# Retention attention with a Mish feed-forward on one core: partition order of the first two tiles' q and k loads, and the place of the first v loads

## The chip, the core and the metric

The kernel runs on one core of a Trainium2 chip. The metric is the device time of one execution in microseconds. Before the change it was 333.55 us, the median of 3 runs (333.04 to 334.23).

A core has TensorE (PE in the profile; its weight loads are PEld), VectorE (DVE), ScalarE (ACT), GpSimd (POOL) and SyncE (SP). Transfers between the off-chip memory and the on-chip buffer run on the core's 16 DMA engines. They are issued here from SP's queue, ACT's queue and POOL's queue.

## What is computed

The inputs are q, k and v of 8 batches, 8 heads, 576 tokens and 64 features, and two weight matrices. The reference, cut to what matters:

```python
scores = (1/sqrt(64)) * q @ k^T                      # per batch and head, 576 x 576
gamma  = 1 - 2 ** (-5 - head)
D[i,j] = gamma ** (i-j) if i >= j else 0
attn   = (scores * D) @ v                            # 576 x 64
x = attn, heads side by side                         # 4608 x 512
h = x @ w_in                                         # 4608 x 2048
g = h * tanh(softplus(h))                            # Mish
out = g @ w_out                                      # 4608 x 512
```

## The kernel before

**Tiles.** The 4608 tokens are cut into 36 chunks of 128, and four chunks make a tile, so there are 9 tiles. Tiles 0 and 1 hold the first 128 tokens of batches 0 to 3 and of batches 4 to 7. They need no state from earlier tokens and have code of their own, the functions whose names begin with `f_`. Chunks 8 to 35 use the general path (`step_p` to `step_o`), with a running state per batch.

**Order of the work.** The schedule is written by hand (`manual_schedule`, L77): every engine executes its instructions in the order in which the program text issues them, and waits only for the data and buffers that it needs.

**First loads of q and k.** `load_rows` (L101) loads q or k of one batch's first 128 tokens, 256 KB, into one plane of a staging buffer with 128 partitions of 512 floats. Eight consecutive tokens of one head go to one partition (2 KB): "(g r)" splits the 128 tokens into g = 16 groups of r = 8. L103 puts the heads outermost, so partition = 16 * head + group. For tile 0 six of these loads are issued from SP (L115: q0, q1, q2, k2, q3, k3) and two from ACT (L117: k0, k1). For tile 1 eight are issued from SP through `load_second_qk` (L105), four when `g1` of tile 0 has reached block f = 6 and four when it has reached f = 12 (L482 to L485). A tiny transfer named `passed` (L484), which reads the result of that block, holds SP's queue until then.

**First loads of v.** `load_first_v` (L110) loads v of one batch's first 128 tokens from POOL's queue, 128 tokens outermost, in pieces of 256 bytes. For batches 0 and 1 it is called at L135, after the distance table `dist`, the identity and `pos`, and before the two causal masks of the general path (`mask`, `mask2`, L137 to L143). The masks are first used by `step_s` (L296), in tile 2.

**From the staging buffer to scores.** `f_cast` (L177) casts two batches of q or k to bf16 and puts them side by side. `f_transpose` (L185) makes eight PE transposes for q and eight for k. Column number c of a transposed block is partition c of the staging buffer; two copies (L192) put the columns into token order per head. `f_scores` (L196) makes q k^T per head and multiplies by the decay `dmask` on DVE. `f_v` (L212) casts v, and `f_out` (L217) multiplies scores by v and copies the result to `xT`. For tile 0 the order is at L434 to L463: casts of batches 0 and 1, their transposes, casts of batches 2 and 3, scores, transposes, outputs, and in between the first four blocks of `g1`.

**POOL's order at the start.** After the masks POOL casts v of batch 0 (L438), which waits for that load, issues the first quarter of w_in (L439), the loads of v 2 and 3 (L441), casts v of batch 1, issues the rest of w_in (L444), casts v of batch 2 (L456), issues w_out (L465), scales v for the states (L467) and then issues v 4 to 7 and the loads of chunks 8 to 11 (L469 to L473).

**Feed-forward.** `g1(t, f)` (L359) multiplies block f of w_in with `xT` of a tile and applies Mish on ACT; there are 16 blocks. `g2_first` (L390) multiplies Mish's result of tile 0 with w_out. Tile 1's attention steps are put between the parts of `g2_first` (L488). From L516 on the general path interleaves the attention of later chunks with `g1` and `g2` of earlier tiles.

Of the kernel before, what the change touches and what calls it, by code (L numbers as in the profile page):

```python
# [17 lines left out]
def kernel(  # L18
# [19 lines left out]
    B, H, S, D = q.shape  # L38
    assert (B, H, S, D) == (8, 8, 576, 64)
    P = 128  # L40
# [59 lines left out]

    def load_rows(queue, t, i, b):  # L101
        queue.dma_start(out=raw[t][i][:, b, :],  # L102
                        in_=(q, k)[i][4 * t + b, :, 0:P, :].rearrange("h (g r) d -> h g (r d)", r=8))  # L103

    def load_second_qk(g):  # L105
        for b in (2 * g, 2 * g + 1):
            for i in range(2):
                load_rows(nc.sync, 1, i, b)

    def load_first_v(b):  # L110
        v0[b] = io.tile([P, H, D], F32, name="vraw", bufs=8)
        nc.gpsimd.dma_start(out=v0[b], in_=v[b, :, 0:P, :].rearrange("h p d -> p h d"))

    for i, b in ((0, 0), (0, 1), (0, 2), (1, 2), (0, 3), (1, 3)):
        load_rows(nc.sync, 0, i, b)  # L115
    for b in range(2):
        load_rows(nc.scalar, 0, 1, b)  # L117
# [14 lines left out]
                   allow_small_or_imprecise_dtypes=True)  # L132
    nc.gpsimd.iota(pos[64:P, 4:5], pattern=[[1, 1]], base=512, channel_multiplier=1,
                   allow_small_or_imprecise_dtypes=True)
    for b in range(2):  # L135
        load_first_v(b)
    mask = consts.tile([P, P], F32)  # L137
    mask2 = consts.tile([P, P], F32)
    nc.gpsimd.memset(mask, 1.0)
# [1 line left out]
                            base=0, pattern=[[1, P]], channel_multiplier=-1)  # L141
    nc.gpsimd.tensor_copy(mask2, mask)
    nc.gpsimd.memset(mask2[0:64, 64:P], 0.0)  # L143
    lg = [math.log(1.0 - 2.0 ** (-5.0 - h)) for h in range(H)]
    dmask = consts.tile([P, H, P], F32)
    for h in range(H):
# [38 lines left out]
    def f_transpose(t, g, copies, tps):  # L185
        for i, name in enumerate(("qb", "kb")):
            for r in range(8):
                nc.tensor.transpose(tps[i][:, r, :], fst[t][name][:, g, r, :, :].rearrange("p x d -> p (x d)"),  # L188
                                    ident)
        for i, name in enumerate(("qb", "kb")):  # L190
            out_t = first.tile([P, H, P], BF16, name=name + "T", bufs=2)
            copies[i](out_t.rearrange("p h (g r) -> p h g r", r=8),  # L192
                      tps[i].rearrange("p r (h g) -> p h g r", h=H))
            fst[t][name, g] = out_t

    def f_scores(t, g):  # L196
# [246 lines left out]
    for i in range(1, 4):  # L443
        load_w_in(512 * i, 512)  # L444
    keep_warm(11)
    f_transpose(0, 0, (act, dve), [ps_h.tile([P, 8, P], BF16, name="hp") for _ in range(2)])
    for i, x in ((0, 0), (0, 1), (1, 0), (1, 1)):
        f_cast(0, i, 1, act, one[x])
    keep_warm(3, ps_sc, "sc")
    f_scores(0, 0)  # L450
    f_transpose(0, 1, (act, act), [ps_st.tile([P, 8, P], BF16, name="st"), ps_o.tile([P, 8, P], BF16, name="ops")])
    f_out(0, 0, act)
    f_out(0, 1, dve)
# [26 lines left out]
    for f in range(4, nF):  # L480
        g1(0, f)
        if f in (6, 12):  # L482
            g = f // 6 - 1
# [5 lines left out]
    for i in range(nF):  # L489
        for step in steps.get(i, "").split():  # L490
            n = int(step[1])
            if step[0] == "T":
                f_transpose(1, n, (dve, act), [ps_sc.tile([P, 2, 8, P], BF16, name="sc")[:, 0] for _ in range(2)])
            elif step[0] == "S":
                f_scores(1, n)
            elif step[0] == "V":
                f_v(1, n, act)
            elif step[0] == "C":
                for j in range(2):
                    f_cast(1, j, n, dve)  # L500
            else:
                f_out(1, n, (dve, act)[n % 2])
        g2_first(i // 4, i % 4)
# [114 lines left out]
```

## Time and profile before

| what | before |
|---|---|
| median of 3 runs | 333.55 us |
| the profiled execution's own time | 335.72 us |
| its span in the profile | 334.0 us |
| PE busy | 306.6 us, 92% of the span |
| PEld, DVE, ACT, POOL busy | 154.6, 137.8, 113.4, 138.8 us |
| mean granted clock of PE | 0.964 |
| DMA traffic | 44.42 MB in 73642 packets |

The profile is one execution. The span is measured from its first to its last event, and the execution's own time is 1.72 us longer. Times inside the profile (a start, a landing) count from the beginning of the span. "Busy" is the time in which an engine executes instructions; a share of DMA is the mean busy share of the 16 DMA engines, so that one half can mean that all are half busy or that half of them are fully busy. It can come out a little above 1. The granted clock is the share of TensorE's full speed that it was given. Queue q1 of the profile carries the DMAs that SP issues, q10 those of ACT, q0 those of POOL, as the issue times and byte counts of the three show.

### The profile page before, as it was taken

The numbers are of one execution on the slowest core, as the hardware profiler recorded it, in microseconds if no ns is written. First come the engines' busy times: TensorE is split into PE (matmuls) and PEld (weight loads), VectorE is DVE, ScalarE is ACT, GpSimd is POOL, SyncE is SP. The second block draws the span as 40 slices with busy tenths as digits, with TensorE's granted clock in tenths as the row PEclk, the third lists the DMA queues.
The fourth block names the chain that finished last, engine by engine and source line by source line (L and its number), as shares of the span: only waits on it lengthen the run. The fifth ranks groups of instructions, "written<-read, shape, count | busy, mean of one in ns | idle before, by whom it ended". The sixth has DMA issues, their size and how long they took to land.

```text
span 334.0 us, 5789 instructions
## 1 busy us (share of the span) xinstructions
PE 306.6 (92%) x2430; PEld 154.6 (46%) x2430; DVE 137.8 (41%) x198; ACT 113.4 (34%) x186; POOL 138.8 (42%) x169
## 2 busy tenths in 40 slices
PE   5568619899999999999999999999999999999996
PEld 1354204445555554545454545455454545444444
DVE  3351003874776474545353545354545433000121
ACT  3376501157623444232322232322222232333300
POOL 5768262919782679482936344452210000000000
PEclk9679956999999999999999999999999999999999
DMA  4899998959985859999999997994061510010022
GB/s 145 239 219 205 252 218 189 180 162 163 163 145 113 150 111 177 200 173 134 179 138 163 152 170 124 154 141 122 31 96 42 87 62 34 31 33 31 31 78 81
DMA packets 73642, 44.42 MB, mean 133 GB/s; under 512 B 58640, under 2 KB 62992, under 8 KB 73616
## 3 DMA queue, kind: packets, MB, share of 16 engines
q0 software_dynamic: 46976, 25.70, 50.0%
q1 hardware_dynamic: 26224, 17.70, 23.8%
q10 hardware_dynamic: 416, 0.66, 0.6%
q8 instruction: 19, 0.31, 0.4%
q14 instruction: 7, 0.06, 0.1%
HBM read 38.80 MB, written 9.44 MB: 144 GB/s over the span
## 4 chain that ended last, share of the span: by engine, by line
PE 84%; DMA 9%; DVE 2%; SPq 1%; ACT 1%; issue 1%; DVEq 0%
PE hp L364 36%; PE ops L379 28%; DMA gT<-in_k_dram 9%; PE hp L379 4%; PE sc L293 2%; PE st L325 2%; PE hp L396 2%; PE sc L345 2%; PE sc L350 2%; SPq L102 1%; DVE kb L182 1%; PE sc L280 1%; PE hp L407 1%; PE ops L396 1%; PE st L396 1%
## 5 line engine op out<-in xcount | busy, mean ns | idle before, releaser
L364 PE MATMUL hp<-xT,w_in_t 128*128 128x512 bf16 (+1 forms) x592 | 144.1, 374 | 1.6 <-DVE xT L231 0.8
L366 ACT ACTIVATE gT<-hp 128x512 bf16<-128x512 f32 (+1 forms) x148 | 86.6, 586 | 155.3 <-PE hp L364 155.1
L379 PE MATMUL ops<-w_out_t,gT 128*128 128x512 bf16 x432 | 110.4, 379 | 0.0
L364 PEld LDWEIGHTS <-w_in_t 128*128 128x128 bf16 x592 | 55.1, 98 | 62.6 <-issue 1.6
L379 PEld LDWEIGHTS <-gT 128*128 128x128 bf16 x496 | 48.3, 98 | 58.0 <-issue 0.8
L415 DVE COPY res<-ops 128x512 f32<-128x512 f32 x28 | 19.3, 688 | 83.3 <-PE ops L379 79.7
L255 POOL DMA_DIRECT2D qraw<-in_q_dram x24 | 22.0, 915 | 51.1 <-DVE qks L265 50.8
L328 DVE TENSOR_TENSOR ssb<-st,diag 128x512 bf16<-128x512 f32 x32 | 21.9, 684 | 47.5 <-PE st L325 47.5
L271 POOL TENSOR_TENSOR vs<-vraw,gv 128x512 bf16<-128x512 f32 x28 | 29.8, 1071 | 20.4 <-issue 13.9
L297 DVE TENSOR_TENSOR sm<-sc,mask 128x1024 bf16<-128x1024 f32 x28 | 33.0, 1214 | 7.1 <-PE sc L293 7.1
L255 POOL DMA_DIRECT2D vraw<-in_v_dram x24 | 21.7, 905 | 8.1 <-DMA qks<-in_k_dram 5.7
L255 POOL DMA_DIRECT2D qks<-in_k_dram x24 | 22.0, 916 | 4.2 <-DMA w_out_t<-in_moe_w_out_dram 1.6
L265 DVE TENSOR_TENSOR qks<-qraw,gq 128x512 bf16<-128x512 f32 x28 | 18.7, 700 | 0.0
L354 DVE CAST xT<-sc 128x512 bf16<-128x512 f32 x24 | 15.3, 680 | 0.0
L379 PE MATMUL hp<-w_out_t,gT 128*128 128x512 bf16 x64 | 15.0, 379 | 0.0
L182 DVE CAST qb<-gT 128x512 bf16<-128x512 f32 (+1 forms) x4 | 2.9, 734 | 26.9 <-DMA gT<-in_q_dram 26.9
L281 ACT COPY qkT<-sc 128x1024 bf16<-128x1024 bf16 x10 | 10.1, 1010 | 8.0 <-PE sc L280 8.0
L259 POOL DMA_DIRECT2D qraw<-in_q_dram x8 | 5.6, 702 | 13.8 <-DVE qks L265 13.8
L188 PEld LDWEIGHTS <-qb 128*128 128x128 bf16 x32 | 2.5, 119 | 17.6 <-DVE qb L182 16.4
L188 PE MATMUL sc<-ident,qb 128*128 128x128 bf16 x16 | 1.6, 263 | 9.8 <-DVE qb L182 9.8
L192 ACT COPY kbT<-sc 128x1024 bf16<-128x1024 bf16 x2 | 2.0, 1012 | 24.8 <-DVE qbT L192 12.5
L396 PEld LDWEIGHTS <-gT 128*128 128x128 bf16 x64 | 6.5, 108 | 8.1 <-issue 2.7
(95 smaller groups left out, 224.8 us busy)
## 6 DMA issues: line engine op xcount, KB each, us to landing
vraw<-in_v_dram POOLq DMA_DIRECT2D x32, 256.0 KB, 7.1
out_dram<-res SPq DMA_DIRECT2D x31, 256.0 KB
qraw<-in_q_dram POOLq DMA_DIRECT2D x24, 256.0 KB, 3.7
qks<-in_k_dram POOLq DMA_DIRECT2D x24, 128.0 KB, 4.4
gT<-in_q_dram SPq DMA_DIRECT2D x8, 256.0 KB
w_in_t<-in_moe_w_in_dram POOLq DMA_DIRECT2D x4, 512.0 KB, 10.3
w_out_t<-in_moe_w_out_dram POOLq DMA_DIRECT2D x4, 512.0 KB, 12.9
gT<-in_k_dram SPq DMA_DIRECT2D x6, 256.0 KB
```

What stands on the lines that cost most here:

```text
L255: nc.gpsimd.dma_start(out=t, in_=src[b, :, ds(P * c, P), :].rearrange("h p d -> p h d"))
L265: nc.vector.tensor_tensor(live[n]["qks"][:, 0], live[n]["q"], gq[:, c, :].unsqueeze(2).to_broadcast([P, H, D]), op=OP.mult)
L271: nc.gpsimd.tensor_tensor(vs, live[n]["v"], gv[:, c, :].unsqueeze(2).to_broadcast([P, H, D]), op=OP.mult)
L281: nc.scalar.copy(qk.rearrange("p i n t -> p (i n) t"), tp)
L297: nc.vector.tensor_tensor(sm.rearrange("p e n i -> p (e n) i"), sc.rearrange("p e n i -> p (e n) i"), m.unsqueeze(1).to_broadcast([P, 2 * ...
L328: nc.vector.tensor_tensor(ssb.rearrange("p e n d -> p e (n d)"), st.rearrange("p n d -> p (n d)").unsqueeze(1).to_broadcast([P, 2, NP * 64 ...
L354: nc.vector.tensor_copy(xts[t][:, :, ts(s, P)], ot)
L364: nc.tensor.matmul(hp[:, cols], lhsT=w_in_t[:, c, ts(f, P)], rhs=xts[t][:, c, cols], start=(c == 0), stop=(c == KC - 1))
L366: nc.scalar.activation(gts[t][:, f, cols], hp[:, cols], AX.Mish)
L379: nc.tensor.matmul(ops, lhsT=gts[t][:, f, ts(s, P)], rhs=w_out_t[:, f, :], start=(f == 0), stop=(f == nF - 1))
L396: nc.tensor.matmul(outs[0, s], lhsT=gts[0][:, f, ts(s, P)], rhs=w_out_t[:, f, :], start=(f == 0), stop=(f == nF - 1))
L415: copy(ot, ops)
```

## The change

Three lines of code change, and two lines move.

1. `load_rows` puts the 16 groups of tokens outermost and the 8 heads within, for all 16 loads of q and k of tiles 0 and 1. The partition is now 8 * group + head. Each piece is still 2 KB and each load still 256 KB.
2. `f_transpose` reads the transposed columns in the new order, "(g h)" instead of "(h g)"; the result in memory is the same.
3. The two calls of `load_first_v` for batches 0 and 1 move behind the four POOL instructions that make the masks.

```diff
     def load_rows(queue, t, i, b):
         queue.dma_start(out=raw[t][i][:, b, :],
-                        in_=(q, k)[i][4 * t + b, :, 0:P, :].rearrange("h (g r) d -> h g (r d)", r=8))
+                        in_=(q, k)[i][4 * t + b, :, 0:P, :].rearrange("h (g r) d -> g h (r d)", r=8))
...
-    for b in range(2):
-        load_first_v(b)
     mask = consts.tile([P, P], F32)
     mask2 = consts.tile([P, P], F32)
     nc.gpsimd.memset(mask, 1.0)
...
     nc.gpsimd.tensor_copy(mask2, mask)
     nc.gpsimd.memset(mask2[0:64, 64:P], 0.0)
+    for b in range(2):
+        load_first_v(b)
...
             copies[i](out_t.rearrange("p h (g r) -> p h g r", r=8),
-                      tps[i].rearrange("p r (h g) -> p h g r", h=H))
+                      tps[i].rearrange("p r (g h) -> p h g r", h=H))
```

## The prediction, made before the changed kernel was run

> **What bounds the kernel now.** I read the page's slices and chain first, then the busy times of chosen stretches, the timeline of the stretches in which PE is not busy, and the traffic of each DMA queue there. Stretches first (us, length, busy time of each engine with its count, granted clock, DMA share, GB/s):
>
> ```profile
> 0.00:8.00 8.00, 4.24 (x11) 1.43 (x11) 3.07 (x23) 2.68 (x4) 4.31 (x16) 1.00 0.48 142
> 8.00:15.00 7.00, 3.68 (x27) 2.24 (x29) 1.93 (x2) 2.06 (x3) 4.84 (x7) 0.51 0.74 222
> 15.00:22.00 7.00, 4.24 (x64) 3.25 (x61) 3.09 (x4) 4.89 (x7) 3.06 (x5) 0.76 1.19 247
> ...
> 38.70:51.60 12.90, 1.87 (x17) 1.61 (x18) 2.28 (x3) 0.60 (x1) 5.68 (x6) 0.64 1.08 220
> 51.60:73.00 21.40, 19.77 (x147) 9.23 (x146) 13.69 (x13) 5.84 (x9) 10.35 (x11) 0.90 0.86 171
> 73.00:283.00 210.00, 210.00 (x1847) 106.09 (x1847) 104.10 (x143) 73.86 (x120) 98.78 (x112) 1.00 0.82 130
> ```
>
> From 73 us on PE is busy for 210.00 of 210.00 us, so whatever brings the work at 73 us forward brings the end forward, and nothing else in the change can. PE's losses lie before 26 us and between 38.7 and 51.6, where it works 1.87 of 12.90 us. The chain of waits says for what:
>
> ```profile
> 4.37 13.63 DMA gT<-in_k_dram
> 18.69 1.05 PE ops L188 x8
> ...
> 34.35 15.58 DMA gT<-in_k_dram
> 50.77 1.04 PE sc L188 x8
> ```
>
> Both long pieces are loads of `load_rows`: the last k of tile 0, landed at 18.0, and the k of tile 1's second batch, landed at 49.95. (The buffer bears the name gT because the staging area is later a gT buffer.) Next, how fast these loads run:
>
> ```profile
> 3.50:5.00 1.50, 1.50 (x6) 0.55 (x5) 0.12 (x2) 1.49 (x2) 1.32 (x4) 1.00 0.53 193
> ...
> 8.00:12.00 4.00, 0.90 (x8) 0.77 (x8) 0.71 (x1) 0.35 (x1) 1.84 (x3) 0.52 0.53 193
> 24.00:32.00 8.00, 7.14 (x56) 4.13 (x55) 1.72 (x3) 4.83 (x11) 7.99 (x9) 1.00 1.24 204
> ```
>
> Between 3.5 and 5 us nothing but q and k moves, many loads are queued, and yet the DMA share stays at 0.53 with 193 GB/s; from 8 to 12 it is the same. A backlog with a share that stands at one half reads as eight engines of sixteen, one for each head of the outermost dimension. POOL's weight loads, with 128 outermost, bring the share to 1.24. So I read the change as doubling the engines of each q and k load, from 8 to 16. The trace has no load with 16 outermost: the bounds are no gain (193 GB/s) and the double (386 GB/s); I take the double, since eight heads gave eight engines and 128 tokens gave all.
>
> The Trainium skill, "DMA: Bandwidth & Descriptors", section "Why a DMA increments its semaphore by 16 and not by 1", says that a DMA uses the largest number of engines up to 16 that divides the slowest dimension of both sides: 8 before, 16 now. Its section "Where 436 GB/s comes from" speaks against the whole double: the memory gives one core about 358 GB/s. By that figure the 2.10 MB of tile 0 take 5.9 us (an estimate from that page) and not 5.4, and the sum would be 0.5 us smaller. Of the stretches of 1 us that I read, the highest is 318 GB/s (15 to 16 us).
>
> **Part 1, tile 0.** Eight loads of 262 KB are 2.10 MB, 10.9 us at 193 GB/s and 5.4 at 386. The timeline of the work behind them:
>
> ```profile
> 10.71 0.78 POOL L86 DMA_DIRECT2D w_in_t<-in_moe_w_in_dram  x1
> ...
> 11.65 0.62 ACT L182 CAST kb<-gT 128x512 bf16<-128x512 f32 x1 [6.28 <-DMA gT<-in_k_dram]
> ...
> 18.02 0.62 ACT L182 CAST kb<-gT 128x512 bf16<-128x512 f32 x1 [1.29 <-DMA gT<-in_k_dram]
> ...
> 20.03 0.61 POOL L214 CAST vb<-vraw 128x512 bf16<-128x512 f32 x1 [3.94 <-DMA vraw<-in_v_dram]
> ...
> 22.68 0.60 ACT L214 CAST vb<-vraw 128x512 bf16<-128x512 f32 x1
> ...
> 26.01 8.36 PE L364 MATMUL hp<-xT,w_in_t 128*128 128x256 bf16 x44 [0.79 <-DVE xT L231]
> ```
>
> By 5.0 us the queues of SP and ACT had moved 0.39 MB. On twice the engines that is 0.78 MB, and 1.24 MB at 6.2 us. Data land about 1 us after the byte counts say (0.26 MB on SP's queue at about 5.6, cast at 6.95). So k1, the fourth of the eight, lands at about 6 instead of 11.65, and the other four, which share the engines with v 0 and 1, between 7.4 and 11.2 instead of 13 to 18. From k1's cast to the scores of batches 0 and 1 took 3.0 us (11.65 to 14.67), then come casts of 0.62, transposes of at most 1.05, copies of 1.01 and 1.22, multiplications of 1.18 each: done one behind the other they bring ACT past the Mish table load (1.28 us, ended 22.56) at about 16.0. That is 6.5 us earlier.
>
> What is late next is v. The masks cost POOL 0.20 + 0.29 + 0.29 + 0.14 = 0.92 us, with gaps 1.13 (4.33 to 5.46), and v's data begin at 6.2 instead of 5.05. v 0 then has q and k beside it on every engine. At half of the 204 GB/s that POOL's queue had alone, its 262 KB take 2.6 us, so it lands at about 9.5 (10.15 before); POOL's cast takes 0.61 and w_in's first quarter is issued near 10.1 (10.71 before). The masks thus cost nothing, since nobody uses them before 73 us and v 0 gains more than they delay it. Behind that quarter stand v 2 and v 3, 1.05 MB in all. They had q and k beside them until 18; now they have the engines to themselves from about 10.5. At 204 to 275 GB/s (24 to 32 us, 12 to 16 us) they need 3.8 to 5.1 us from about 11.8, and land at about 17, with 1 us of lag. v 3's cast on ACT starts at about 17.2 instead of 22.68, and the row at 26.01, from which PE works almost without a gap to 38.7, follows. **Part 1: -5.5 us**, bounds -4 (v 3 at 18.7) and -7 (q and k alone decide). The next quarters of w_in land every 2.6 us (0.52 MB at 204) from about 19.6; g1 needs one per 4 blocks x 0.865 us = 3.5 us, so they hold nothing up.
>
> **Part 2, tile 1.** The loads begin when g1 of tile 0 has reached f = 6 and compete with w_out, v 4 to 7 and the chunk loads:
>
> ```profile
> 32.32 0.63 SPq L102 DMA_DIRECT2D gT<-in_q_dram  x1
> ...
> 36.75 0.58 SPq L484 DMA_DIRECT2D passed<-gT  x1
> ...
> 50.02 0.69 DVE L182 CAST kb<-gT 128x1024 bf16<-128x1024 f32 x1 [1.60 <-DMA gT<-in_k_dram]
> ```
>
> Issued at 32.32, landed at 50.0: 17.7 us for 1.05 MB. SP's queue moved almost nothing until 36 (3.7 us), then 0.40 MB to 41.5, which is 73 GB/s or 9.1 per engine. On 16 engines that is 145 GB/s: 3.7 + 7.2 + 1 of lag = 11.9 us, 5.8 less. If both queues got half of each engine (12 of 24 GB/s), it is 3.7 + 5.5 + 1 = 10.2, 7.5 less. I take 6.2, near the measured rate. PE reaches the end of tile 0's g1 6.4 us after the issue, so it still waits some 4 to 5 us. The second four loads follow at the same rate and land some 19 us after the first issue; their casts stood at 59.4, 27 after it, and come to stand 21 after. They fit, by little. **Part 2: -6.2**, bounds -4 and -7.7.
>
> **Part 3, PE's clock.** The granted clock was 0.50 from 43 to 55, and some ten matmuls after 51.6 took 0.43 us instead of 0.22: 2.1 us. It fell 3.7 us after PE stopped. With a wait of 4 to 5 us, cut by the transposes of q, it may fall or not: I take **-1.0**, bounds 0 and -2.1.
>
> **Nothing.** The copies of L192 keep their 1024 elements per partition, and only the step between columns changes: DVE 1.22, ACT 1.01 us. If they cost or saved a fifth, the eight copies, three on the chain, move the end by 0.7 us. SP's issues keep 0.6 us each. From 73 us on POOL's loads have slack: chunk 11's were issued by 60, and PE needs it at about 84; they also come earlier, since POOL had sat up to 5.7 us on transfers that shared engines with q and k.
>
> **Sum.** -5.5 - 6.2 - 1.0 = -12.7 us on the profiled span of 334.0 (321.3), which its own time exceeds by 1.72. The median of the runs is 333.55, 2.17 below the profiled execution; the difference carries over: 320.8 us.
>
> **The rivals.**
> - *More of it.* Queues share evenly and the wait is too short for the clock to fall: -7 - 7.5 - 2.1 = -16.6, 317.0 us. For it: engines of 24 GB/s were at 9 beside POOL's traffic in a stretch that also ended waits of POOL. Against: all three ends at once. Chance 0.14.
> - *Tile 0 gives little.* v 0 has q and k on all its engines and lands no earlier; w_in and v 2, v 3 follow late, and only 1 to 2 us remain of part 1: -1.5 - 5.8 = -7.3, 326.2 us. For it: POOL's cast of v 0 already waited 4.70 us. Chance 0.16.
> - *The loads stay on eight engines*, because sixteen groups are not spread as I read it. Then only v's delay acts: q and k have the engines alone 1.1 us longer, v 0 comes about 1 later: 333.5 us within 1. Chance 0.04.
> - *Slower.* Pieces of 2 KB from eight distant heads run at half of each engine's rate, so 16 engines carry 193 GB/s, and they take it from v 0 on every engine instead of eight. Then q and k end near 13, v 0 lands near 15, w_in is issued 5 later, v 3 lands near 25 and its cast comes 2 later than 22.68: 335.6 us. It decides where v 0 lands more than about 3 us later than 10.15. Against: the slowest row with all engines, 204 GB/s, is above 193. Chance 0.04.
>
> **Numbers.** My forecast has 0.62. Its own range is 318 to 324. The range for 8 in 10 reaches into the first two rivals: 315.5 to 327.5. Faster by over 0.3% (about what a measurement of this kernel can tell from no change) has 0.62 + 0.14 + 0.16 = 0.92, the same 0.04, slower 0.04.
>
> **What would show it.** DMA share near 1 and over 300 GB/s between 3.5 and 5 us; k1's cast near 6 to 7, the last k's near 11; v 0's cast at 9 to 10; g1's long run from about 20.5; tile 1's k cast about 12 us after its first load's issue; PE busy without a gap from about 60. I am wrong if the share stays at 0.53, if v 0 lands after 11, or if PE waits in the general path because chunk loads come late.

## The result, and the profile after

The changed kernel took 324.64 us, the median of 4 runs, where the old one took 333.44 us: 8.8 us less. The ratio of the two kernels is 0.9717 (95% interval 0.9672 to 0.9762). Ratios here compare only runs that count as fast, which leaves out this kernel's run of 329.06 us and one later run of the old kernel (527.5 us). Measured a second time the changed kernel took 327.21 us against 333.85, a ratio of 0.9781 (0.9730 to 0.9832). The ten runs of these two measurements lie between 323.0 and 329.1 us; their standard deviation is 2.2 us, against 1.1 us for the old kernel's 47 runs (332.2 to 337.3).

The first stretches of the changed kernel's profile, with the columns of before (us, length, busy time of each engine with its count, granted clock, DMA share, GB/s), have the same bounds as the first three rows shown of the old kernel; the last three are cut at the new events:

```profile
0.00:8.00 8.00, 5.14 (x14) 1.75 (x15) 3.92 (x24) 3.30 (x5) 4.50 (x16) 1.00 0.75 191
8.00:15.00 7.00, 6.51 (x59) 4.42 (x56) 3.58 (x3) 4.70 (x7) 3.75 (x6) 1.00 0.79 183
15.00:22.00 7.00, 5.52 (x56) 3.69 (x56) 3.32 (x4) 4.85 (x10) 6.19 (x9) 1.00 1.20 239
...
35.10:41.30 6.20, 1.95 (x18) 1.65 (x18) 2.32 (x3) 0.60 (x1) 0.90 (x1) 0.70 1.14 302
41.30:60.20 18.90, 18.57 (x143) 8.95 (x143) 10.32 (x13) 5.84 (x9) 15.86 (x17) 0.92 1.32 251
60.20:270.50 210.30, 208.72 (x1818) 106.30 (x1848) 104.79 (x143) 74.07 (x120) 98.81 (x112) 1.00 0.83 134
```

The stretch between tile 0's `g1` and `g2_first`, in which PE mostly stands and does little but tile 1's first transposes, has shrunk from 12.9 us (38.7 to 51.6) to 6.2 us (35.1 to 41.3), and the general path, which began at 73 us, begins at 60.2. From there to the end it is 261.1 us in both profiles, so nothing is given back. (PE shows as busy for 208.72 of the 210.30 us; the row has 1818 matmuls and 1848 weight loads, so records of matmuls are missing.) The span fell from 334.0 to 321.3 us, which is exactly the forecast's figure, but the median fell by 8.8 us and not by 12.7. Most of the study is about that difference.

The loads of q and k themselves, in the same view of the changed kernel:

```profile
3.50:5.00 1.50, 1.50 (x5) 0.48 (x4) 0.28 (x5) 1.31 (x3) 1.44 (x4) 1.00 1.07 279
8.00:12.00 4.00, 3.96 (x37) 2.58 (x35) 1.22 (x1) 2.63 (x4) 0.76 (x2) 1.00 0.99 273
12.00:14.00 2.00, 1.56 (x14) 1.29 (x15) 1.93 (x2) 1.29 (x2) 2.00 (x3) 1.00 0.25 9
```

The share between 3.5 and 5 us went from 0.53 to 1.07, as 16 engines instead of 8 would show, but the rate only from 193 to 279 GB/s. The third row is new: from 12 to 14 us there is next to no traffic (9 GB/s, where the old kernel has 263).

The chain of waits, its long pieces (start, length, what) in the changed kernel:

```profile
3.71 7.48 DMA vraw<-in_v_dram
...
13.46 5.21 DMA vraw<-in_v_dram
...
30.62 8.96 DMA gT<-in_k_dram
```

In the old kernel the first long piece was k's last load. It is now v 0's load, then v 3's; for tile 1 it is still k, with 8.96 instead of 15.58 us. The timeline of the changed kernel says the same with the instructions that answer to those shown of before:

```profile
11.24 0.61 POOL L214 CAST vb<-vraw 128x512 bf16<-128x512 f32 x1 [5.58 <-DMA vraw<-in_v_dram]
11.80 0.77 POOL L86 DMA_DIRECT2D w_in_t<-in_moe_w_in_dram  x1
...
12.71 0.62 ACT L182 CAST kb<-gT 128x512 bf16<-128x512 f32 x1 [1.28 <-DMA gT<-in_k_dram]
...
17.21 1.89 PE L364 MATMUL hp<-xT,w_in_t 128*128 128x256 bf16 x8 [0.59 <-DMA w_in_t<-in_moe_w_in_dram]
...
18.69 0.62 ACT L214 CAST vb<-vraw 128x512 bf16<-128x512 f32 x1 [1.22 <-DMA vraw<-in_v_dram]
...
22.47 12.67 PE L364 MATMUL hp<-xT,w_in_t 128*128 128x256 bf16 x63 [0.79 <-DVE xT L231]
...
28.73 0.55 SPq L102 DMA_DIRECT2D gT<-in_q_dram  x1
...
39.67 0.69 DVE L182 CAST kb<-gT 128x1024 bf16<-128x1024 f32 x1 [0.67 <-DMA gT<-in_k_dram]
```

The last k is cast at 12.71 instead of 18.02. But v 0 is cast at 11.24 instead of 10.15, and w_in's first quarter is issued at 11.80 instead of 10.71. PE waits for it at 17.21 (0.59 us), a wait that the old kernel did not have.

### The profile page after: what moved, and what is told of

Same layout as the page of the kernel before. It is cut to its first block, busy times and chain, and to the rows that moved or that the text cites. A ratio compares the mean times of both kernels' runs of the same rounds, so it can differ in the third digit from the quotient of the medians.

```text
span 321.3 us, 5751 instructions
## 1 busy us (share of the span) xinstructions
PE 306.2 (95%) x2392; PEld 155.6 (48%) x2430; DVE 135.8 (42%) x198; ACT 113.6 (35%) x186; POOL 138.8 (43%) x169
## 4 chain that ended last, share of the span: by engine, by line
PE 88%; DMA 7%; POOL 1%; issue 1%; DVE 1%; SPq 0%; ACT 0%; POOLq 0%; DVEq 0%
PE hp L364 37%; PE ops L379 29%; PE hp L379 4%; DMA vraw<-in_v_dram 4%; DMA gT<-in_k_dram 3%; PE hp L396 2%; PE sc L293 2%; PE st L325 2%; PE sc L345 2%; PE sc L350 2%; PE sc L280 1%; PE st L396 1%; PE ops L396 1%; PE hp L407 1%; PE sc L188 1%
## 5 line engine op out<-in xcount | busy, mean ns | idle before, releaser
L364 PE MATMUL hp<-xT,w_in_t 128*128 128x512 bf16 (+1 forms) x562 | 142.6, 377 | 3.3 <-DVE xT L231 0.8
L271 POOL TENSOR_TENSOR vs<-vraw,gv 128x512 bf16<-128x512 f32 x28 | 29.8, 1073 | 20.4 <-issue 13.9
L345 PE MATMUL sc<-qkT,ssb 128*64 128x128 bf16 (+1 forms) x224 | 9.5, 213 | 0.0
L350 PE MATMUL sc<-sm,vs 128*64 128x128 bf16 x192 | 9.4, 219 | 0.0
L241 POOL DMA_DIRECT2D k<-in_k_dram x8 | 7.3, 915 | 4.4 <-DMA w_out_t<-in_moe_w_out_dram 4.4
```

Source lines behind the costliest of these rows:

```text
L271: nc.gpsimd.tensor_tensor(vs, live[n]["v"], gv[:, c, :].unsqueeze(2).to_broadcast([P, H, D]), op=OP.mult)
L345: nc.tensor.matmul(ot[ds(64 * e, 64), p, ds(i0, iw)], lhsT=st_sb[bb, cc][:, e, p, :], rhs=qk[:, 0, p, ds(i0, iw)], start=(i0 == 0 and p == ...
L350: nc.tensor.matmul(ot[ds(64 * e, 64), p, :], lhsT=vs[:, 2 * p + e, :], rhs=sm[:, e, p, :], start=False, stop=True, skip_group_check=True)
L364: nc.tensor.matmul(hp[:, cols], lhsT=w_in_t[:, c, ts(f, P)], rhs=xts[t][:, c, cols], start=(c == 0), stop=(c == KC - 1))
```

## The experiments

**The theory and its rivals.** The theory: the gain is that each load of q and k runs on 16 engines instead of 8, once at tile 0 and once at tile 1; the move of v's loads gives part of it back, because POOL issues w_in and the next v loads only after v 0 has landed. One rival: v out of the way is what lets q and k come early. Another: not the engines, but the order of the pieces is what is fast.

The events of one profile of each kernel (the first, where there are more) are set side by side here, in us from the start of the span. "v 0", "v 3" and "last k" are the starts of these casts for tile 0 (where the view puts two casts of k into one row, that row's start; the last cast then starts about 0.5 us later); "run" is the start of PE's long run of `g1`; "loads" is the time from the first issue of a tile 1 load to the cast of tile 1's first k; "path" is the first `g1` of tile 1, where the general path begins. The last column is the median of the runs.

| kernel | last k | v 0 | v 3 | run | loads | path | span | us |
|---|---|---|---|---|---|---|---|---|
| old | 18.02 | 10.15 | 22.68 | 26.01 | 17.7 | 72.94 | 334.0 | 333.44 |
| changed | 12.71 | 11.24 | 18.69 | 22.47 | 10.9 | 60.23 | 321.3 | 324.64 |
| order only (v ahead of the masks) | 12.57 | 9.61 | 17.76 | 21.08 | 11.3 | 59.71 | 320.8 | 321.89 |
| v's move only | 16.68 | 10.96 | 21.04 | 24.36 | 18.4 | 70.52 | 331.6 | 332.72 |
| new order in tile 0 only | 12.77 | 11.53 | 19.20 | 23.75 | 18.6 | 69.19 | 330.3 | 332.01 |
| new order in tile 1 only | 16.91 | 11.06 | 21.57 | 25.04 | 12.8 | 65.40 | 326.5 | 327.25 |
| two half loads | 19.47 | 11.51 | 24.14 | 27.82 | 17.9 | 72.44 | 333.5 | 335.46 |
| rows in one piece | 9.41 | 10.32 | 17.79 | 22.23 | 10.9 | 60.37 | 321.4 | 323.15 |
| w_in first | 13.05 | 11.36 | 17.71 | 21.34 | 11.8 | 59.43 | 320.5 | 322.16 |
| order only, earlier release | 12.79 | 9.76 | 17.97 | 21.30 | 10.7 | 56.45 | 317.5 | 319.34 |
| the same, w_in first | 13.54 | 9.53 | 17.89 | 21.22 | 10.3 | 54.90 | 316.0 | 317.73 |

In every row the span is the column "path" plus 261.0 to 261.1 us. What happens before tile 1's `g1` is the whole of the difference, in all of them.

### The new order without the move of v

```diff
+    for b in range(2):
+        load_first_v(b)
     mask = consts.tile([P, P], F32)
...
     nc.gpsimd.memset(mask2[0:64, 64:P], 0.0)
-    for b in range(2):
-        load_first_v(b)
```

> The loads of q and k have groups outermost, as in the changed kernel, and v's first loads stand before the masks again, as in the old one. Theory (the number of DMA engines per load makes the whole gain, and the move of v costs a little, because v 0 landed at 11.2 instead of 10.15 and w_in's first quarter is issued after it): v is issued 1.4 us earlier, v 0 lands near 10 and the time is 323.5 us, some 1 us below the changed kernel's 324.6. Rival (v out of the way is what brings q and k early): k's last load of tile 0 lands 2 us later than 12.7, and the time is 326.5 or more.

Measured: 321.89 us, 0.9654 of the old kernel (0.9614 to 0.9694). It is 2.7 us faster than the changed kernel, more than the theory expected. v 0 is cast at 9.61 and the hole from 12 to 14 us is gone. The DMA queues of that window, first in the changed kernel (queue, packets, MB, share of 16 engines):

```profile
q0 software_dynamic: 18, 0.02, 24.9%
```

and in the kernel with v ahead of the masks:

```profile
q0 software_dynamic: 309, 0.32, 105.7%
```

POOL's queue (q0) moved 0.32 MB there and 0.02 in the changed kernel. The last k was not 2 us later: the row with the last two casts of k starts at 12.57 and ends at 13.70, so the last one starts near 13.1, where the changed kernel's starts at 12.71. So the rival falls: v beside q and k costs them little, and v late costs the weights.

### The move of v without the new order

```diff
-    for b in range(2):
-        load_first_v(b)
     mask = consts.tile([P, P], F32)
...
     nc.gpsimd.memset(mask2[0:64, 64:P], 0.0)
+    for b in range(2):
+        load_first_v(b)
```

> The heads are outermost, as in the old kernel, and v's first loads stand behind the masks. Theory (engines): 333.5 us, within 1 of the old kernel; the DMA share between 3.5 and 5 us stays at 0.53. Rival (v out of the way): at least 3 us of the gain, 330.5 or less.

Measured: 332.72 us, 0.9974 (0.9954 to 0.9994), and the share between 3.5 and 5 us is 0.53. The move alone thus gains some 0.9 us. Here the last k came 1.3 us earlier (16.68), and v 3's cast 1.6 us earlier (21.04), although v 0 came 0.8 later. With q and k on eight engines the move gains a little, with the new order it costs 2.7 us: its sign depends on the other part of the change.

### One tile at a time

```diff
-                        in_=(q, k)[i][4 * t + b, :, 0:P, :].rearrange("h (g r) d -> g h (r d)", r=8))
+                        in_=(q, k)[i][4 * t + b, :, 0:P, :].rearrange("h (g r) d -> g h (r d)" if t == 0 else "h (g r) d -> h g (r d)", r=8))
...
-                      tps[i].rearrange("p r (g h) -> p h g r", h=H))
+                      tps[i].rearrange("p r (g h) -> p h g r" if t == 0 else "p r (h g) -> p h g r", h=H))
```

For tile 1 alone the condition is `t == 1`.

> Groups outermost for the loads of tile 0 alone; tile 1's keep heads outermost; v behind the masks. Theory (two separate gains, part 1 about 3.5 us and part 2 about 6.8 with 2.3 that follow it): 333.4 - 3.5 = 329.9 us, and tile 1's k cast still stands 17 to 18 us after its first load's issue. Rival (the gain at tile 0 is lost in the wait for tile 1's loads): 333.

Measured: 332.01 us, 0.9954 (0.9925 to 0.9983), 1.8 us less and not 3.5. The long run starts 2.3 us before that of the old kernel's profile, tile 1's k cast only 1.4: the loads took 18.6 us from their issue instead of 17.7. Beside the kernel with v's move alone, which is what this edit adds to, the medians differ by 0.7 us. So there is something in the rival: as these times read, an earlier start of tile 0's `g1` issues tile 1's slow loads earlier, and some of it is lost in the wait for them.

> Groups outermost for the loads of tile 1 alone; v behind the masks. Theory (two separate gains): 333.4 - 6.8 - 2.3 = 324.3 by the profile's terms, and 326 if the terms of the median are as much smaller as the median's gain was (8.8 instead of 12.7); tile 1's k cast stands 11 us after its first load's issue. Rival (tile 1's gain comes from the earlier finish of tile 0, by which POOL's queue is emptier): 331 or more, and the cast stands 16 us or more after the issue.

Measured: 327.25 us, 0.9818 (0.9793 to 0.9843), 6.6 us less; the k cast stands 12.8 us after the first issue. The rival is refuted: tile 1's loads gain by their own order. Most of the change's gain is tile 1's.

### Is it the engines, or the order of the pieces?

```diff
-        queue.dma_start(out=raw[t][i][:, b, :],
-                        in_=(q, k)[i][4 * t + b, :, 0:P, :].rearrange("h (g r) d -> g h (r d)", r=8))
+        for x in range(2):
+            queue.dma_start(out=raw[t][i][ds(64 * x, 64), b, :],
+                            in_=(q, k)[i][4 * t + b, :, ds(64 * x, 64), :].rearrange("h (g r) d -> g h (r d)", r=8))
```

> Each load of q and k is cut into two, of the first 64 and the last 64 tokens. Groups are outermost and heads within, so that every byte lands where the changed kernel puts it, but each load has 8 groups outermost instead of 16. Theory (the size of the outermost dimension sets the number of engines): DMA share near 0.53 and about 190 GB/s between 3.5 and 5 us, the last k of tile 0 at 17 to 19 us, 332 to 335 us in all. Rival (the order of the pieces, spread over the eight heads and over all partitions, is what is fast): share near 1, and 324 to 326 us.

Measured: 335.46 us, 1.0039 (1.0007 to 1.0072). Every byte goes to the same place as in the changed kernel, from the same places and in pieces of the same size, and yet the gain is gone. Its stretch from 3.5 to 5 us:

```profile
3.50:5.00 1.50, 1.50 (x5) 0.48 (x4) 0.25 (x4) 0.99 (x1) 1.44 (x4) 1.00 0.54 186
```

The share is back at 0.54. Eight groups outermost give half of the engines, as eight heads did, and sixteen give all. These loads are also half as large and go to 64 partitions each, but neither was so in the old kernel, which has the same share. The rule in the Trainium skill, "DMA: Bandwidth & Descriptors", section "Why a DMA increments its semaphore by 16 and not by 1", that the slowest dimension of both sides sets the number of engines, agrees with the three kernels: 8 heads, 0.53; 8 groups, 0.54; 16 groups, 1.07. Twice the issues, which end SP's first series at 11.6 us instead of 5, go with the 1.5 us by which this kernel is slower than the old one; that part was not taken out by itself.

### Why 279 GB/s and not 386

```diff
-                        in_=(q, k)[i][4 * t + b, :, 0:P, :].rearrange("h (g r) d -> g h (r d)", r=8))
+                        in_=(q, k)[i][4 * t + b].rearrange("h s d -> (h s) d")[0:1024].rearrange("(p r) d -> p (r d)", r=8))
```

> Each load of q and k takes 256 KB that lie in one piece in memory, the first 128 x 512 numbers of its batch, instead of 8 tokens each from 8 heads: other rows of q and k are loaded than the reference uses, and the amount is the same. The changed kernel's 16 engines moved 260 to 280 GB/s between 3.5 and 8 us, 17 per engine, and not the 386 that was forecast. Theory (a limit that all engines share): 260 to 280 GB/s here too. Rival (16 engines are slowed by pieces from eight distant heads): over 330 GB/s between 3.5 and 8 us, and the last k of tile 0 lands 1 to 2 us before 12.7.

Measured: 323.15 us in one run, with other rows than the reference needs, so this kernel serves only to measure. The stretches are:

```profile
3.50:5.00 1.50, 1.50 (x7) 0.47 (x5) 1.19 (x7) 0.94 (x3) 1.44 (x4) 1.00 1.05 355
5.00:8.00 3.00, 1.89 (x20) 1.11 (x19) 1.81 (x3) 1.88 (x3) 0.79 (x1) 1.00 0.95 314
8.00:12.00 4.00, 2.61 (x40) 1.84 (x40) 2.76 (x3) 3.37 (x6) 1.68 (x3) 0.86 0.44 157
```

The same amount in one piece moves at 355 GB/s instead of 279, with about the same share of the engines. So 279 is no limit that all engines share: the way the pieces are gathered slows them, as the rival had it. This load also differs in having 128 partitions and not 16 groups outermost, so which of the two it is stays open. The Trainium skill's figure of about 358 GB/s that the memory gives one core ("DMA: Bandwidth & Descriptors", section "Where 436 GB/s comes from") lies just above these 355; the changed kernel's own loads do not come near it.

The other half of this run matters more. The last casts of k were done from 9.41 on, some 3 us earlier than in the changed kernel, and the time is within the changed kernel's runs. The share from 8 to 12 us is 0.44: after q, k, v 0 and v 1 have landed nothing is queued, because POOL issues w_in's first quarter only at 10.88, behind its cast of v 0 (10.32). Of the 3 us little reaches PE. The long run starts 0.2 us earlier than in the changed kernel's first profile. In its other two TensorE's clock was half before the long run, as here (eight matmuls of `g1` take 1.87 us), and beside them it starts 1.3 to 1.4 us earlier.

### POOL does not wait for v 0

```diff
-    f_v(0, 0, pool)
     load_w_in(0, 512)
     for b in (2, 3):
         load_first_v(b)
+    f_v(0, 0, pool)
     f_v(0, 1, pool)
```

> The changed kernel, with POOL's issues of w_in's first quarter and of v 2 and v 3 ahead of its cast of v 0, which waits for v 0's landing at 11.2. Theory (tile 0 is now bound by what POOL issues only after v 0 has landed; from 12 to 14 us the DMA share was 0.25): the hole closes, w_in's first quarter lands near 14.5 instead of 17.2, v 3 near 16.5 instead of 18.7, PE's long run starts 2 us before 22.47, and the time falls by about 2 us, to 322.6. Rival (these transfers take the engines from q and k): the last k of tile 0 lands 2 us later than 12.7, and the time stays within 1 us of the changed kernel's.

Measured: 322.16 us, 0.9659 (0.9622 to 0.9697), 2.5 us below the changed kernel's first median, and four runs within 0.4 us. (The two profiled runs, 322.25 and 323.0, differ by less, since the changed kernel's was its fastest.) The hole is filled:

```profile
12.00:16.00 4.00, 2.16 (x28) 1.73 (x30) 1.42 (x3) 2.74 (x4) 3.04 (x5) 0.56 1.17 260
```

(DMA share 1.17, where the changed kernel had 0.71.) The last k is 0.3 us later, not 2. In the profile the long run came only 1.1 us earlier, not 2, since v 3 was 1.0 us earlier and not 2. With the run above this shows the mechanism from both sides: what is late at tile 0 in the changed kernel is what POOL issues after v 0's landing. That taking POOL's wait away gains is clear, how much of the 2.5 us is due to it is not.

### Once more, on one chip

> The changed kernel once more, beside the next three on one chip. Theory (the old kernel's profile was some 2 us above its median and the changed one's was the fastest of its runs, so that the medians' difference of 8.8 us is the true one and the spans' 12.7 is not): 324.0 to 325 us. Rival (the spans are right and the first few runs were disturbed): 321 to 322.5 us.

Measured: 327.21 us, even slower than the theory expected; the rival that the spans are right falls. Its profiled run took 324.84 us, with a span of 323.1.

> Groups outermost and v's first loads ahead of the masks, once more. Theory (with the new order the move of v costs time, since w_in's first quarter and v 2 and v 3 are issued only after v 0 has landed, at 11.2 instead of 9.6): 1.5 to 2.7 us below the changed kernel of the same call. Rival (the difference of 2.7 us between the first two measurements was chance): within 0.5 us of it.

Measured: 321.47 us, 0.9620 (0.9581 to 0.9659), 5.7 us below the changed kernel beside it. It was 2.7 between the first measurements, which were not made together. The sign is certain; the size varies with the changed kernel's own spread.

> As the kernel with v ahead of the masks, but tile 1's loads of q and k are released after blocks 4 and 8 of tile 0's g1 instead of 6 and 12. Theory (PE still stands some 4 us for tile 1's loads, which need 10.9 us from the issue whatever comes before): they are issued 1.7 us earlier, PE waits 1.7 us less, and the time is about 1.7 us below that of the kernel with v ahead of the masks, near 320. Rival (the loads take engines from w_out and POOL's queue, which then lands later): no gain, within 0.5 us.

```diff
-        if f in (6, 12):
-            g = f // 6 - 1
+        if f in (4, 8):
+            g = f // 4 - 1
```

Measured: 319.34 us, 0.9570 (0.9525 to 0.9615), 2.1 us below the kernel with v ahead of the masks. The loads took 10.7 us from their first issue, and that was 1.5 us earlier than in the first profile of the kernel with v ahead of the masks and 1.2 earlier than in its second; the theory had 1.7.

> As the kernel before it, with w_in's first quarter and v 2 and v 3 issued ahead of POOL's cast of v 0. Theory (with v early the hole in the transfers is already closed: the DMA share from 12 to 16 us was 1.12 with v ahead of the masks): within 0.7 us of the kernel before it. Rival (POOL's wait for v 0 still costs as much as it did with v behind the masks, where taking it away gave 2.5 us): 1.5 us or more below it.

Measured: 317.73 us, 0.9523 (0.9483 to 0.9563), 1.6 us below. This is the rival's figure and not the theory's. But the rival's cause, POOL's wait for v 0, is not shown by it: in the two profiles the long run starts within 0.1 us (21.30, 21.22), and the path 1.55 us earlier. Of these, 0.4 are shorter loads and 1.0 lie behind tile 1's k cast; in this run the transposes of tile 1's k took 0.62 and not 1.04 us, so TensorE's clock had not fallen. Whether the issue order or the clock gives the 1.6 us was not separated. It is the fastest version of the study, faster than both kernels.

> The changed kernel a third time, for one more profile: its ten runs so far lie between 323.0 and 329.1, those of the kernel with v ahead of the masks between 320.2 and 322.5, and both profiles so far are of runs below 325. Theory (the spread comes from TensorE's clock, which stayed at 1.00 in tile 0 in the first profile and stood at 0.50 from 15 to 22 us in the second): a time above 326 goes with a half clock both in tile 0 and before 45 us, and with PE's long run starting after 24. Rival (a stall like that of the old kernel's profile, where one DVE cast took 3.98 us instead of 1.05): the long run starts between 22.4 and 23.7 and a single instruction is late by 3 us.

Measured: 325.04 us, on another chip. The run was not one of those above 326, so it decides nothing on them; it repeats the second profile (run at 23.57, clock 0.50 from 15 to 22 us, span 323.3).

## Why the prediction was right in its sign and too large in its size

- **The engines: right.** The share doubled, and the half loads show that the outermost dimension does it. The signs that followed came too: k1's cast at 6.26, tile 1's k cast 10.9 us after the first issue, the general path from 60.23.
- **"I take the double": wrong.** 386 GB/s was the forecast, 279 came. Last k's cast was at 12.71 instead of the 11.2 forecast for its landing. By itself this cost the total little, 1.4 us at most, as the run with rows in one piece shows.
- **"The masks thus cost nothing, since nobody uses them before 73 us and v 0 gains more than they delay it": this is the step that failed.** v 0 did not land at about 9.5 but at 11.2, and "if v 0 lands after 11" was among the forecast's own signs of being wrong. The term that failed is the start of v's data, put at 6.2 us: it was 9.0. Of POOL's queue the changed kernel shows nothing from 6 to 9 us; the only queue with traffic is SP's, on all engines, where the old kernel's POOL queue moved 0.28 MB. The rows from 6 to 7 us, the changed kernel's only one and the old kernel's for POOL's queue:

```profile
q1 hardware_dynamic: 143, 0.26, 106.8%
...
q0 software_dynamic: 41, 0.14, 47.6%
```

From the issue of v 0 to its first data it takes 2.8 to 3.0 us in all four kernels whose loads of tile 0 run on eight engines (the old one, v's move only, new order in tile 1 only, half loads), and 4.0 to 5.5 us in all others, where they run on sixteen; in the changed kernel's three profiles it is 5.2 to 5.5. Once the data flow, v 0 is there after 2.2 us, where the forecast had 3.3 from 6.2 to 9.5. So what delays v 0 is not a slow transfer beside q and k but a longer wait for its first data, and that wait goes with the sixteen engines. How an engine chooses between the queues no run shows. Behind its cast POOL holds w_in's first quarter, v 2 and v 3, and these, not q and k, end tile 0. With v ahead of the masks v 0 was cast at 9.61, and the time was 321.89 and 321.47 us: 11.9 and 12.4 below the old kernel beside them. So the new order alone brings about the -12.7 of the forecast, which is partly luck, since the forecast was for both parts of the change. The move of v gave 2.7 us of it back in one measurement and 5.7 in the other. The rival *tile 0 gives little* had named that mechanism; it had priced tile 0 too low and put 326.2 us, close to the second median.
- **Part 1, -5.5 us:** the long run came 3.5 us earlier in the first profile and 2.4 in the other two. It is 4.9 and 5.3 with v ahead of the masks. That is nearly the forecast's -5.5, which did not count v's delay.
- **Part 2, -6.2 us: right.** The loads took 10.9 us from the first issue instead of 17.7: -6.8. The two other kernels with the old order at tile 1 have 18.4 and 18.6.
- **Part 3, the clock, -1.0 us: wrong.** PE waited 3.9 us and the clock fell as before; eight matmuls after 41.25 took 0.43 us instead of the ten of the old kernel, a gain of about 0.4 instead of 1.0.
- **The carry from the span to the median: wrong.** It took over to the medians what was a difference of two profiles. But the two profiled runs stand differently among the runs of their kernels: the old one's (335.72) is 2.3 us above its kernel's median, the changed one's (323.0) 1.6 below, and 8.8 + 2.3 + 1.6 = 12.7. Of the old kernel's 47 runs 43 were shorter than the profiled one. Its profile has a row that is far longer than its like in the others:

```profile
60.39 3.98 DVE L182 CAST kb<-gT 128x1024 bf16<-128x1024 f32 x1
```

In the profile of the kernel with v's move only, which has the same code from there on, the row is

```profile
59.35 1.05 DVE L182 CAST kb<-gT 128x1024 bf16<-128x1024 f32 x1
```

From tile 1's k cast to the path took 22.9 us in the old kernel's profile, and 21.5 and 20.6 us in the two kernels that keep its loads there. So some 1.5 to 2.3 us of the spans' difference of 12.7 (3.5 + 6.8 + 2.4) go with this row, as far as these profiles tell. Whether it is chance is open. In the old kernel's profile this cast meets POOL's multiplication of v (L271, from 60.96 for 2.05 us), and the only other profile where the two overlap, that of the new order in tile 1 only, has 1.97 us for the same cast; in all others it takes 0.67 to 1.05. That the two hinder each other fits this, but no run tested it. The spans' agreement with the forecast was a sum of errors that cancelled: part 1 was 2.0 us too large, and this row, which the forecast did not have, about made up for it.

**The spread of the changed kernel.** Part of it is TensorE's clock at tile 0. Three rows of the changed kernel's second profile:

```profile
11.09 0.62 PE L188 MATMUL st<-ident,qb 128*128 128x128 bf16 x8 [0.20 <-ACT qb L182]
...
19.99 1.86 PE L364 MATMUL hp<-xT,w_in_t 128*128 128x256 bf16 x8 [0.56 <-ACT gT L366]
21.79 0.64 PE L228 MATMUL st<-gT,vb 128*64 128x128 bf16 x8
```

and the same three of its first:

```profile
11.91 1.03 PE L188 MATMUL st<-ident,qb 128*128 128x128 bf16 x8
...
19.65 1.47 PE L364 MATMUL hp<-xT,w_in_t 128*128 128x256 bf16 x8 [0.55 <-ACT gT L366]
21.04 0.41 PE L228 MATMUL st<-gT,vb 128*64 128x128 bf16 x8
```

In the second the transposes ran fast at 11 us, and the clock had fallen when `g1` began: eight of its matmuls took 1.86 us, and eight of `f_out` 0.64. In the first it was slow at 12 us and rose near 20.5 (0.41). From v 3's cast to the long run this makes 4.60 instead of 3.78 us. It explains 0.8 of the 1.8 us between the two spans. Where the runs between 326 and 329 us lose their time is open: none of them was profiled. A slower clock alone does not explain them, since the two runs of 329.06 us have a mean granted clock of 0.984, and the profiled runs near 325 have 0.974. No kernel with v ahead of the masks, or with POOL not waiting for v 0, had a run more than 2.4 us above its median.

## What to carry to other kernels

A load whose outermost dimension is 8 keeps half of the DMA engines idle; reorder its access pattern so that 16 or more stands outermost, and look at the DMA share while many loads are queued to see whether it does. When you move a transfer behind cheap instructions, count what its queue issues only after it has landed: four instructions of 0.14 to 0.32 us cost this kernel 3 to 6 us, because weights and the next loads of v were queued behind a wait for the moved load. And before you carry a difference of two profiles to medians, see where each profiled run stands among the runs of its kernel.

## What the runs showed of the hardware that was not expected

- Sixteen engines moved 279 GB/s in pieces of 2 KB from eight heads, 17 per engine, where eight engines moved 193, 24 per engine, and sixteen moved 355 with rows in one piece. The share of busy time, 1.05 to 1.07, does not tell the two kinds of load apart.
- While loads of SP's and ACT's queues ran on all 16 engines, the first load of POOL's queue moved its first data 4.0 to 5.5 us after its issue; while they ran on eight, 2.8 to 3.0.
- The column of the granted clock can be wrong before its first change. The changed kernel's first profile has 1.00 in every stretch up to 37 us, yet eight transposes at 11.91 took 1.03 us, as at a clock of 0.50, and the eight at 11.09 of the second profile took 0.62. The durations decide.
